# A recurrence and a mixer on one core: four turned tiles in the place of six, PE operations cut finer, loads shared between two queues, and new lists of order

## The chip, the cores and the metric

The kernel runs on one core of a Trainium2 chip. The metric is the device time of one execution in microseconds (us). Five engines work in parallel, each through its own list of instructions in order, and wait for each other by semaphores: TensorE (PE in the profile; PEld is its loading of weights), VectorE (DVE), ScalarE (ACT), GpSimd (POOL) and SyncE (SP), which only issues transfers. PE writes to PSUM, eight banks of 128 x 512 float32; DVE and ACT read it from there.

## The reference

```python
for t in range(S):                     # B, H, S, D = 4, 8, 768, 40
    y[:, :, t] = einsum('bhd,bhde->bhe', rt, state)
    Sa = einsum('bhde,bhe->bhd', state, at)
    state_decay = state * wt[:, :, None, :] - einsum('bhd,bhe->bhde', Sa, bt)
    state = state_decay + einsum('bhd,bhe->bhde', vt, kt)
x = y.transpose(0, 2, 1, 3).reshape(B, S, H * D)          # 4 x 768 x 320
theta = x @ w_theta
y = einsum('ts,bsd->btd', w_tok_r, x * cos(theta)) \
  + einsum('ts,bsd->btd', w_tok_i, x * sin(theta))
u = x + y
out = u + maximum(u @ w_ch, 0)
```

All inputs and the output are float32. Each head of each batch has a 40 x 40 state that runs through 768 steps; then a mixer over tokens and channels works on all heads of a batch together.

## The kernel before

The 768 steps of a batch are cut into 6 tiles of 128, so there are 24 tiles (i = 0 to 23, a batch after the other), and in each tile the recurrence is written as products of matrices. All 8 heads of a tile are worked on at once. The steps of tile i, by the names that the code gives its operations:

- `loads` (line 462): w, k, b, a, v of the tile into SBUF, as 1024 pieces of 160 bytes each. r of two tiles is loaded at once, in 256 pieces of 1280 bytes, "runs" of eight steps of a head. v is loaded in runs too for tiles 0 to 7 (`RUNS`, where the operation is called o), and k, b and a for the "turned" tiles 0 to 5 (`TURNED`). There are 25 loads of runs. All these loads are issued by SP.
- `prep` (line 503): logarithm of w on ACT, its running sums by a matmul with a triangle (`cs`; for tiles under `LATE` = 12 a second matmul gives the sums up to the step before), exponentials on ACT. In tiles that aren't turned, POOL multiplies k and b (`kb`, one operation of 640 columns) and a (`ah`) by these decays, and PE transposes the three (`tt`, 12 blocks, with v 16), which ACT or DVE copies out of PSUM (`et`) as features. In turned tiles POOL or ACT casts the raw runs (`ck`, `cb`, `ca`), PE transposes those (`tkbr`, `tar`) for two tiles at once, forms the sums transposed (`csT`), ACT takes two more exponentials of 512 columns (`xi`, `xw`), DVE makes the features by three products (`mk`, `mb`, `ma`), and PE transposes k and b back (`tbk`, copied by `ebk`).
- `attention_scores` (line 684): three products of features on half-arrays, each of 128 x 1024 results, which DVE multiplies by a mask (`mpsi`, `mphi`, `mlv`). The other way: ACT copies them with a sign and POOL sets the masked part to zero (`sel`). A fourth (`mlu`) follows from the recurrence.
- `recurrence` (line 694): `x0` adds the older state's part and the tile's own in one PSUM bank, `nx` copies it, `nu` continues in the same bank, `gt` forms the next state, which DVE scales (`egt`); `gd` and `nut` are transposes.
- `readout` (line 824): `y`, of the older state's part and two parts of scores, and DVE's product into x.
- The mixer: `theta` transposes x of two tiles, `sines` multiplies by w_theta, ACT takes sine and cosine, POOL or DVE makes the products z; `mix_row` is 6 chunks of 2 matmuls (`row`) over the tiles of a batch for each of its 6 rows, then the addition of x (`uadd`), a transpose, the channel product (`ch`) and the store.

A matmul works on the whole array of 128 rows or on half of it (64 rows, two at a time). `turn` (line 416) transposes by halves, `turn_whole` (line 422) by whole blocks; scores, `th3` and `ch3` use halves.

The program doesn't plan while it is built. Every operation is added to a list of 1390 with what it reads and writes; `ORDER` gives the order in which they are put on their engines, `HOMES` the PSUM banks, `PICK` (134 numbers) those which take their other form (ACT in the place of DVE or POOL, the other transpose, and so on), and `WARM` places matmuls on constants at the start. As every engine works in order, `ORDER` also sets what stands behind a waiting operation. The figures `cost` and `work` in the code have no part in what is built.

Of the kernel before, what the change touches and what calls it, by code (L numbers as in the profile page):

```python
# [19 lines left out]
TURNED = frozenset(range(6))  # L20
LATE = 12
ORDER = [
# [218 lines left out]
def mm(n):  # L241
    return max(n / 2.4 + 2.5, 25.0)
# [7 lines left out]
def kernel(  # L250
# [252 lines left out]
    def prep(i):  # L503
# [12 lines left out]
        def cs():  # L516
# [7 lines left out]
            if late:  # L524
                return
# [517 lines left out]
```

## Time and profile before

| | |
|---|---|
| time, median of 3 runs (lowest, highest) | 194.6 us (194.04, 196.16) |
| profiled execution: span from first to last instruction | 191.6 us |
| profiled execution: its own time | not given beside the span |
| mean granted PE clock | 0.991 |
| PE matmuls | 4223 |
| transfers | 30.90 MB in 110312 packets |

In the profile a line such as `L668 PE MATMUL ps<-feat ... x384 | 18.4, 221 | 1.9 <-ACT exi L611 0.9` is a group of instructions: line of the code, engine, operation, what it writes and reads, how often, busy us in all, mean ns of one, and the idle time of the engine just before them with what ended it. A line of a wait list gives who waited for whom: us in all, times, longest. A line of a table by stretch gives start and end, then the stretch's length and the busy us (and instructions) of PE, PEld, DVE, ACT and POOL, the granted clock, the DMA engines' busy share and GB/s. In the chain of work a piece is start, us, and what. The busy time of PE has modelled ends: matmuls overlap.

### The profile page before, as it was taken

To read this page: it belongs to the slowest core of one execution; us is meant where nothing else is said; L and a number is where in the kernel's file an instruction comes from. 1 tells how busy PE (TensorE), PEld (TensorE's weight loads), DVE (VectorE), ACT (ScalarE), POOL (GpSimd) and SP (SyncE) were. 2 spreads that over 40 slices of the span, in tenths; PEclk is the share of its full clock that TensorE was granted. 3 is DMA by queue.
4 is the path that set the end of the run, shared out by engine and by line. 5 is a ranking of instruction groups with operands and counts; after the bars stand their busy time and mean duration, and the time that the engine had idled before them with its cause. 6 is when DMAs were issued, how large, how long until landed. Compare 5 with 4: busy or idle time off the path is not lost.

```text
span 191.6 us, 9477 instructions
## 1 busy us (share of the span) xinstructions
PE 179.6 (94%) x4223; PEld 142.0 (74%) x4223; DVE 165.7 (86%) x268; ACT 157.9 (82%) x288; POOL 136.9 (71%) x162
## 2 busy tenths in 40 slices
PE   7679799999898999999999999999999999999992
PEld 7567587787687877788777787868877877876751
DVE  7599899998899998999889978998999998886552
ACT  3499999999999999989999979799999769883010
POOL 5584595496799789989989396694999983643200
PEclk9969999999999999999999999999999999999999
DMA  5999799989889999999997999999927011001131
GB/s 131 321 310 323 182 244 205 178 150 160 164 137 211 187 187 174 201 215 193 197 207 171 154 191 210 179 169 238 217 38 168 12 37 38 3 3 68 68 140 68
DMA packets 110312, 30.90 MB, mean 161 GB/s; under 512 B 98624, under 2 KB 110272, under 8 KB 110272
## 3 DMA queue, kind: packets, MB, share of 16 engines
q1 hardware_dynamic: 107840, 27.53, 66.6%
q0 software_dynamic: 2432, 2.77, 9.1%
q8 instruction: 33, 0.54, 1.1%
q14 instruction: 7, 0.06, 0.1%
HBM read 29.13 MB, written 3.93 MB: 173 GB/s over the span
## 4 chain that ended last, share of the span: by engine, by line
PE 74%; DVE 13%; ACT 7%; DMA 2%; issue 1%; SPq 1%; POOL 0%; ACTq 0%
PE ps L896 22%; PE ps L419 12%; PE ps L668 10%; PE ps L810 6%; DVE lam L676 4%; PE ps L842 4%; PE ps L424 3%; DMA raw_a<-in_a_dram 2%; PE ps L745 2%; PE ps L816 2%; PE ps L724 2%; PE ps L712 2%; PE ps L836 2%; PE ps L707 2%; PE ps L518 2%; DVE feat L625 2%
## 5 line engine op out<-in xcount | busy, mean ns | idle before, releaser
L676 DVE TENSOR_TENSOR lam<-ps,mask_p 128x1024 bf16<-128x1024 f32 x39 | 47.1, 1219 | 3.6 <-PE ps L668 3.3
L896 PE MATMUL ps<-z,wtok 128*128 128x320 bf16 x288 | 48.2, 299 | 0.0
L493 POOL TENSOR_TENSOR z<-cs,xp 128x640 bf16<-128x640 f32 x21 | 29.2, 1403 | 4.5 <-ACT cs L874 4.4
L896 PEld LDWEIGHTS <-wtok 128*128 128x128 bf16 x288 | 24.3, 97 | 9.1 <-issue 0.2
L493 POOL TENSOR_TENSOR kb<-raw_kb,ex 128x640 bf16<-128x640 f32 x18 | 25.8, 1433 | 2.0 <-ACT nx L718 1.3
L676 DVE TENSOR_TENSOR psi<-ps,mask_p 128x1024 bf16<-128x1024 f32 x19 | 23.1, 1219 | 1.1 <-PE ps L668 1.0
L668 PEld LDWEIGHTS <-feat 64*128 64x128 bf16 x576 | 18.0, 95 | 6.6 <-issue 4.4
L668 PE MATMUL ps<-feat 64*128 64x128 bf16 x384 | 18.4, 221 | 1.9 <-ACT exi L611 0.9
L676 DVE TENSOR_TENSOR phi<-ps,mask_n 128x1024 bf16<-128x1024 f32 x13 | 15.9, 1220 | 1.6 <-PE ps L668 1.6
L680 POOL TENSOR_SCALAR_AFFINE_SELECT phi<-phi 128x1024 bf16<-128x1024 bf16 x11 | 12.0, 1092 | 7.0 <-ACT phi L678 7.0
L842 PE MATMUL ps<-kb,lam 128*128 128x40 bf16 x384 | 15.5, 180 | 0.2 <-DVE lam L676 0.2
L452 ACT COPY feat<-ps 128x1024 f32<-128x1024 f32 (+1 forms) x14 | 14.0, 998 | 0.6 <-PE ps L419 0.5
L842 PEld LDWEIGHTS <-lam 128*128 128x128 bf16 x384 | 13.8, 96 | 0.8 <-issue 0.3
L642 ACT COPY rT<-ps 128x512 bf16<-128x512 bf16 x24 | 13.3, 600 | 0.3 <-PE ps L419 0.2
L509 ACT ACTIVATE lw<-raw_w 128x320 bf16<-128x320 f32 x24 | 11.4, 483 | 2.4 <-DMA raw_w<-in_w_dram 2.3
L680 POOL TENSOR_SCALAR_AFFINE_SELECT lam<-lam 128x1024 bf16<-128x1024 bf16 x9 | 9.8, 1090 | 4.9 <-ACT lam L678 4.9
L901 DVE TENSOR_TENSOR up<-ps,xp 128x320 bf16<-128x320 f32 x22 | 10.6, 487 | 2.8 <-PE ps L896 2.5
L493 POOL TENSOR_TENSOR ah<-raw_a,ex 128x320 bf16<-128x320 f32 x15 | 12.1, 806 | 0.7 <-ACT ex L544 0.4
L452 ACT COPY uT<-ps 128x320 f32<-128x320 f32 (+1 forms) x9 | 3.6, 404 | 10.8 <-PE ps L419 5.4
L678 ACT ACTIVATE phi<-ps 128x1024 bf16<-128x1024 f32 x11 | 11.4, 1033 | 1.0 <-PE ps L668 1.0
L836 PE MATMUL ps<-gd,rT 128*128 128x80 bf16 x80 | 12.2, 197 | 0.0
L728 ACT ACTIVATE nu<-ps 128x320 bf16<-128x320 f32 x24 | 10.8, 450 | 1.5 <-PE ps L724 1.2
(165 smaller groups left out, 538.4 us busy)
## 6 DMA issues: line engine op xcount, KB each, us to landing
raw_w<-in_w_dram SPq DMA_DIRECT2D x24, 160.0 KB, 4.7
raw_r<-in_r_dram SPq DMA_DIRECT2D x12, 320.0 KB, 5.0
out_dram<-oo SPq DMA_DIRECT2D x11, 320.0 KB, 3.1
raw_a<-in_a_dram SPq DMA_DIRECT2D x18, 160.0 KB, 4.5
raw_kb<-in_k_dram SPq DMA_DIRECT2D x18, 160.0 KB, 4.2
raw_kb<-in_b_dram SPq DMA_DIRECT2D x18, 160.0 KB, 4.4
raw_v<-in_v_dram SPq DMA_DIRECT2D x16, 160.0 KB, 5.0
raw_v<-in_v_dram SPq DMA_DIRECT2D x4, 320.0 KB, 5.7
```

The lines of the kernel that those rows point to most:

```text
L419: nc.tensor.transpose(out=dst[:, c, n * 64:n * 64 + 64], in_=block[rows(c)], identity=ident[rows(c), rows(c)])
L452: nc.scalar.copy(out=to, in_=source)
L493: pool = ("POOL", lambda: nc.gpsimd.tensor_tensor(out=dst, in0=in0, in1=in1, op=ALU.mult))
L509: add("ACT", "ln", i, lambda: nc.scalar.activation(out=heads(lw)[:, :, 0:D], in_=raw_w[s4], func=AF.Ln), 473, [("raw_w", s4)], [("lw", s2) ...
L642: add("ACT", "e" + nm, i + x, lambda x=x, dst=dst: nc.scalar.copy(out=dst.rearrange("p g (t q) -> p g t q", q=8), in_=ps(pr).bitcast(BF16) ...
L668: nc.tensor.matmul(t[:, q, g, :], lhsT=lhs[rows(q), g, :], rhs=rhs[rows(q), g, :], start=True, stop=True)
L676: add("DVE", kindm, i, lambda: nc.vector.tensor_tensor(out=flat, in0=whole(), in1=mask.to_broadcast([128, 2 * G, 128]), op=ALU.mult), 1217 ...
L680: add(None, "sel", i, None, 0, dkeys, dkeys, alts=(("POOL", lambda: nc.gpsimd.affine_select(out=flat, in_=flat, pattern=[[0, 2 * G], [1, 1 ...
L810: nc.tensor.matmul(ps(pk)[:, c, 0:DM], lhsT=lhs[:, 3 * c + kt, :], rhs=wt[:, 3 * c + kt, :], start=kt == 0, stop=False, skip_group_check=True)
L836: nc.tensor.matmul(t[:, g * 80:g * 80 + 80], lhsT=rT[:, g, :], rhs=gd[:, 2 * g:2 * g + 2, :], start=True, stop=False, skip_group_check=True)
L842: nc.tensor.matmul(t[:, h * D:h * D + D], lhsT=lam[:, n, p, g, :], rhs=kb[:, n, h, 0:D], start=first and n == 0, stop=n == 1, skip_group_c ...
L896: nc.tensor.matmul(ps(pk)[:, 0:DM], lhsT=wtok[t % NCH][:, c, s, :], rhs=z[:, c, s], start=s == 0 and c == 0, stop=s == NT - 1 and c == 1)
```

## The change

- `TURNED` holds tiles 0 to 3, not 0 to 5. Tiles 4 and 5 load k, b and a in pieces of 160 bytes and go the other way (products on POOL, `tt`).
- Operations of PE are cut finer, with the same matmuls: `tt` into a part for k and b, one for a and one for v; `cs` into its two matmuls' parts; `x0` into the tile's own part and the older state's (`x0s`); `gt` into the part of k and v (`gtk`) and the part of nu; `y` into `yv`, `ys` and `y`. There are 1512 operations.
- Loads of runs have a second form, issued by POOL. There are 22 of them now, and `PICK` takes this form for 13: r of tiles 2, 4, 6, 8, 10, 14, 16 and 18, v of tiles 0, 2, 4 and 6, a of tile 2.
- `ORDER`, `HOMES`, `PICK` (145 numbers) and `WARM` are new lists.
- Another way to cut the blocks of x and u (`SIDES`, `SLOT`) is in the code, for no tile: `SIDES` is empty.

```diff
-TURNED = frozenset(range(6))
+TURNED = frozenset(range(4))
+SIDES = frozenset()
...
-WARM = {14: (38, 0), 19: (10, 3), 20: (2, 3), 62: (4, 3)}
+WARM = {14: (38, 0), 20: (10, 0), 21: (2, 2), 64: (4, 4)}
...
-    def turn(dst, blocks):
-        for n, block in enumerate(blocks):
+    def turn(dst, blocks, at=0):
+        for n, block in enumerate(blocks, at):
...
+        if groups:
+            m = 0
+            for c, (count, keys) in enumerate(groups):
+                add("PE", kind + "abc"[c], i, lambda m=m, count=count: turn(
+                    ps(p).bitcast(BF16), blocks[m:m + count], m), reads=keys, writes=[p],
+                    at=at, new=(p, 2) if c == 0 else None, **quad_cost(4 * count))
+                m += count
...
             add("SP", "load" + nm, i, lambda to=raw, runs=runs: nc.sync.dma_start(
-                out=to, in_=runs), 600, [], [run_key(nm, i, 0), run_key(nm, i, 1)], work=1040)
+                out=to, in_=runs), 600, [], [run_key(nm, i, 0), run_key(nm, i, 1)], work=1040,
+                alts=(("POOL", lambda to=raw, runs=runs: nc.gpsimd.dma_start(
+                    out=to, in_=runs)),))
...
-            if late:
-                return
+
+        def earlier():
             before = lw[:, LEAD - 1:LEAD - 1 + H * 64].rearrange("p (h x) -> p h x", x=64)
...
+        if not late:
+            add("PE", "csx", i, earlier, mm(328), [("lw", s2)], [pk], tail=tail(328))
...
-        skeys, dkeys = [("kb", i % NKB), ("ah", i % 3)], list(parts)
+        groups, dkeys = [(8, [("kb", i % NKB)]), (4, [("ah", i % 3)])], list(parts)
...
         def x0():
             t = ps(pk)
+            for h in range(H):
+                nc.tensor.matmul(t[:, h * D:h * D + D], lhsT=psi[:, h % 2, h // 2, :],
+                                 rhs=vb[:, h, 0:D], start=h == 0, stop=True,
+                                 skip_group_check=True)
+
+        def carried():
+            t = ps(pk)
             for g in range(G):
...
+                nc.tensor.matmul(t[:, g * 80:g * 80 + 80], lhsT=feat[:, 8 + g, :],
+                                 rhs=gt_old[:, g, :, 0:D], start=False, stop=True,
+                                 skip_group_check=True)
+        add("PE", "x0", i, x0, 8 * 25, [("psi", i % NSC), ("v", i % NRV)], [pk], new=(pk, 1),
+            tail=tail(40))
+        if not first:
+            add("PE", "x0s", i, carried, 4 * mm(80), [("fa", st), ("gt", (i + 1) % 2)], [pk],
+                tail=tail(80))
...
+            add("PE", "gtk", i, lambda: gains(kb[:, 0], vb, True),
+                4 * mm(80) + (mm(320) if join else 0), [("kb", i % NKB), ("v", i % NRV)] +
                 ([("gt", (i + 1) % 2)] if join else []), [gk], new=(gk, 1), tail=tail(80))
+            add("PE", "gt", i, lambda: gains(kb[:, 1], nu, False), 4 * mm(80),
+                [("kb", i % NKB), ("nu", s2)], [gk], tail=tail(80))
...
+        add("PE", "yv", i, lambda: y(0), 8 * 25, [("lam", s2, 0), ("kb", i % NKB)], [pk],
+            new=(pk, 1), tail=tail(40))
+        if not first:
+            add("PE", "ys", i, carried, 4 * mm(80), [("rT", i % 6), ("gd", (i + 1) % 2)], [pk],
+                tail=tail(80))
+        add("PE", "y", i, lambda: y(1), 8 * 25, [("lam", s2, 1), ("kb", i % NKB)], [pk],
+            tail=tail(40))
```

The new lists, from the start of the list of order on, begin for SP with w0, b0, k0, a0, w1, r0, w2, k2, w3, b2, w4 and for POOL, behind the casts of tile 0's b and k, with the loads of v of tile 0, a of tile 2 and v of tile 2.

More of the change, by code (lines that the diff above doesn't have):

```diff
@@ L427, in quad_cost, with turned @@
         return dict(mode=64, tail=tail(64), cost=n * 8)
-    def turned(kind, kinde, i, blocks, skeys, dst, dkeys, at="tile", eng="ACT", part=64):
+    def turned(kind, kinde, i, blocks, skeys, dst, dkeys, at="tile", eng="ACT", part=64,
+               groups=()):
         p = ("ps", kind, i)
@@ L432, in turned @@
         whole = n <= 8
-        add("PE", kind, i, lambda: turn(ps(p).bitcast(BF16), blocks), reads=skeys, writes=[p],
-            at=at, new=(p, 2), alts=(("PE", lambda: turn_whole(ps(p).bitcast(BF16), blocks)),)
-            if whole else (), **quad_cost(4 * n))
+        if groups:
[5 more added lines that the diff above has]
+                m += count
+        else:
+            add("PE", kind, i, lambda: turn(ps(p).bitcast(BF16), blocks), reads=skeys,
+                writes=[p], at=at, new=(p, 2),
+                alts=(("PE", lambda: turn_whole(ps(p).bitcast(BF16), blocks)),)
+                if whole else (), **quad_cost(4 * n))
         def places(width, source):
@@ L528, in cs @@
                              rhs=before[:, :, 0:D + 1], start=True, stop=True)
-        add("PE", "cs", i, cs, (1 if late else 2) * mm(328) + 4 * 25, [("lw", s2)], [pk],
-            new=(pk, 1 if late else 2), tail=tail(2 if late else 328))
+        add("PE", "cs", i, cs, mm(328) + 4 * 25, [("lw", s2)], [pk],
+            new=(pk, 1 if late else 2), tail=tail(2))
+        if not late:
+            add("PE", "csx", i, earlier, mm(328), [("lw", s2)], [pk], tail=tail(328))
         if late:
@@ L704, in x0 @@
             t = ps(pk)
-            for g in range(G):
-                if not first:
-                    nc.tensor.matmul(t[:, g * 80:g * 80 + 80], lhsT=feat[:, 8 + g, :],
-                                     rhs=gt_old[:, g, :, 0:D],
-                                     start=g == 0, stop=False, skip_group_check=True)
-                for p in range(2):
-                    h = 2 * g + p
-                    nc.tensor.matmul(t[:, h * D:h * D + D], lhsT=psi[:, p, g, :],
-                                     rhs=vb[:, h, 0:D], start=first and h == 0,
-                                     stop=True, skip_group_check=True)
-        add("PE", "x0", i, x0, 8 * 25 + (0 if first else 4 * mm(80)),
-            [("fa", st), ("psi", i % NSC), ("v", i % NRV)] +
-            ([] if first else [("gt", (i + 1) % 2)]), [pk], new=(pk, 1), tail=tail(40))
+            for h in range(H):
[4 more added lines that the diff above has]
+            t = ps(pk)
+            for g in range(G):
+                nc.tensor.matmul(t[:, g * 80:g * 80 + 80], lhsT=feat[:, 8 + g, :],
[6 more added lines that the diff above has]
+                tail=tail(80))
         add("ACT", "nx", i, lambda: nc.scalar.copy(out=nx, in_=ps(pk)[:, 0:DM]),
@@ L773, in recurrence, with blocks_of @@
                nuT_t[i % 2], [("nuT", i % 2)])
-    def blocks_of(t):
+    def blocks_of(t, sides=False):
+        if sides:
+            split = t.rearrange("p (c k d) -> p k c d", c=2, d=64)
+            return [split[:, kt] for kt in range(5)]
         return [t[:, m:m + 128] for m in range(0, t.shape[1], 128)]
@@ L797, in mixed, with sides @@
         pk = ("ps", kind, q)
+        if not alone(q) and q in SIDES:
+            def sides():
+                for kt in range(5):
+                    for c in range(2):
+                        nc.tensor.matmul(ps(pk)[:, c, 0:DM], lhsT=lhs[rows(c), kt, :],
+                                         rhs=wt[rows(c), SLOT[c][kt], :], start=kt == 0, stop=kt == 4,
+                                         skip_group_check=True)
+            add("PE", kind, q, sides, 5 * mm(320), [lkey] + wkeys, [pk], at=at, new=(pk, 2),
+                tail=tail(320), mode=64)
+            return
         if alone(q):
```

48 lines of the change are left out of this document (21 added, 27 removed), and 212 rows, old and new, of tables (HOMES, ORDER, PICK).

## The prediction

> **What bounds the kernel now.** I read the page first, then busy time by stretch, then who waited for whom in each stretch, then the chain of work.
>
> ```profile
> span 191.6 us, 9477 instructions
> PE 179.6 (94%) x4223; PEld 142.0 (74%) x4223; DVE 165.7 (86%) x268; ACT 157.9 (82%) x288; POOL 136.9 (71%) x162
> 0.00:10.00 10.00, 7.29 (x124) 6.45 (x124) 6.34 (x44) 4.48 (x7) 5.77 (x21) 1.00 0.81 230
> 10.00:68.50 58.50, 53.13 (x1500) 43.99 (x1501) 55.60 (x73) 56.88 (x111) 43.37 (x52) 0.97 1.01 204
> 68.50:187.00 118.50, 118.06 (x2597) 91.09 (x2593) 102.74 (x150) 96.26 (x171) 87.73 (x91) 1.00 0.67 138
> PE ps L419 <- DVE us L901: 0.4, 1, 0.4
> 68.51 0.20 PE L707 MATMUL ps<-gt,feat 128*128 128x80 bf16 x1
> ```
>
> By the page TensorE (PE) is 94% busy, but that is a mean over two different stages. The stretches (columns: PE, PEld, DVE, ACT, POOL busy, granted clock, DMA share) part them. From 68.5 to 187 PE is busy for 118.06 of 118.5 us, and the wait list of that stretch for PE has one entry, 0.4 us: nothing but the amount of PE work sets its length. From 10 to 68.5 PE idles 5.4 us while ScalarE (ACT) is busy 56.88 of 58.5 and VectorE (DVE) 55.60; GpSimd (POOL) idles 15.1. I cut at 68.5 because there PE begins tile 9's state product (line 707), a point found in both lists of order.
>
> ```profile
> ACT exw L613 <- DVE feat L628: 1.0, 1, 1.0
> ACT ex L544 <- PE ps L527: 0.3, 1, 0.3
> POOL phi L680 <- ACT phi L678: 5.9, 4, 2.9
> POOL r L499 <- DMA raw_r<-in_r_dram: 1.4, 1, 1.4
> 8.09 0.47 ACT L509 ACTIVATE lw<-raw_w 128x320 bf16<-128x320 f32 x1 [1.02 <-DMA raw_w<-in_w_dram]
> ```
>
> In the early stretch ACT's longest wait is 1.0 us, once: it works through its list almost without pause, and PE gets results at ACT's pace. So the end is, nearly, the time at which ACT reaches tile 9, plus the PE work behind that point, plus 4.6 us of tail. Work taken from ACT ahead of tile 9 is worth its full length; work taken from PE counts behind tile 9; the rest is covered.
>
> **PE work.** The finer operations issue the same matmuls as before (12 for a state product, 20 for an output, 8 for a state update). Three things do change.
>
> ```profile
> 102.22 0.33 PE ps L668 x8
> 110.97 0.22 PE ps L668 x8
> 109.62 0.56 PE ps L896 x4
> 115.52 0.65 PE ps L896 x4
> 123.38 1.13 PE ps L419 x70
> L604 PE MATMUL ps<-ntri_inc,lw 128*128 128x128 bf16 x24 | 2.3, 219 | 0.0
> ```
>
> These are pieces of the chain. Eight score matmuls on half-arrays (64 rows) take 0.33 us behind whole-array matmuls and 0.22 behind half-array ones; four mixing matmuls take 0.65 against 0.56. So each change between the two array modes costs PE some 0.10 us. Reading both lists in order, PE changes mode 166 times before and 172 after: +0.6 us. The Trainium skill, TensorEngine Tiling (Array Packing), Key Properties, says that changing the tiling mode drains TensorE; it speaks against cutting operations finer, states no price, and the rows agree on the direction. Two tiles fewer are turned: 40 blocks (80 half transposes) go and 24 blocks (48) come, 32 x 16 ns (1.13 us for 70) = -0.5 us, and 8 of line 604's matmuls go. Each costs between 28 ns (0.22 us for eight of the same width on half-arrays) and its own length of 219; I take twice 28, since they fill the whole array: -0.45. Whole-array transposes are picked 33 times, not 32: +0.1. Sum -0.25 us, between -1.6 and 0; behind tile 9, where no tile is turned and the lists hold nearly the same PE work, I count -0.1.
>
> **ACT and DVE ahead of tile 9.** I counted each kind of operation that the two lists put ahead of that point.
>
> ```profile
> L613 ACT ACTIVATE exw<-ps,sign_col 128x512 f32<-128x512 f32 x6 | 4.2, 698 | 1.2 <-DVE feat L628 1.0 <-PE ps L745 0.2
> L611 ACT ACTIVATE exi<-ps 128x512 f32<-128x512 f32 x6 | 3.6, 601 | 0.0
> L678 ACT ACTIVATE phi<-ps 128x1024 bf16<-128x1024 f32 x11 | 11.4, 1033 | 1.0 <-PE ps L668 1.0
> L452 ACT COPY nuT<-ps 128x256 f32<-128x256 f32 x15 | 5.6, 376 | 1.0 <-PE ps L419 0.9
> L452 ACT COPY feat<-ps 128x768 f32<-128x768 f32 (+1 forms) x2 | 1.8, 916 | 0.2 <-PE ps L419 0.2
> L452 ACT COPY gd<-ps 128x160 f32<-128x160 f32 x9 | 2.8, 312 | 0.6 <-PE ps L419 0.4 <-PE ps L424 0.2
> L452 ACT COPY xT<-ps 128x320 f32<-128x320 f32 x7 | 3.1, 436 | 0.4 <-PE ps L419 0.4
> L718 ACT CAST nx<-ps 128x320 bf16<-128x320 f32 x24 | 10.4, 434 | 1.3 <-PE ps L712 1.0
> L874 ACT ACTIVATE cs<-ps 128x640 f32<-128x640 f32 (+1 forms) x13 | 8.7, 666 | 2.6 <-PE ps L801 2.6
> L625 DVE TENSOR_TENSOR feat<-ps,exi 128x512 bf16<-128x512 bf16 x12 | 7.9, 682 | 1.6 <-PE ps L419 1.6
> L456 DVE COPY kb<-ps 128x1024 bf16<-128x1024 bf16 x4 | 2.7, 680 | 0.0
> L676 DVE TENSOR_TENSOR phi<-ps,mask_n 128x1024 bf16<-128x1024 f32 x13 | 15.9, 1220 | 1.6 <-PE ps L668 1.6
> L456 DVE COPY nuT<-ps 128x512 bf16<-128x512 bf16 x9 | 3.8, 419 | 0.6 <-PE ps L419 0.6
> L456 DVE COPY wtok<-ps 128x1536 bf16<-128x1536 bf16 x2 | 1.9, 948 | 0.0
> ```
>
> ACT loses the two exponentials of tiles 4 and 5 (2 x 0.698 + 2 x 0.601 = 2.6), three score copies net (3.1), three copies of nuT (1.1), two of gd (0.6) and a logarithm (0.47); it gains three feature copies (3 x about 0.8 = 2.4, below the mean of two sizes), three casts of 640 columns, which ACT never does in this trace (between 0.434 for 320 columns and twice that; 0.7 each, 2.2), and a sine and a copy of xT (0.7 + 0.4): -2.2 us in instruction lengths. Lengths overlap: over the whole list they add up to 178 us against 157.9 busy, a factor 0.89, so **-1.95 us**. One of the casts (tile 0's a) can stand in the 1.02 us hole ahead of tile 2's logarithm at 8.09, for a further **-0.6** (0 if the cast is late itself). DVE loses six decay products and two copies (5.5), two copies of wtok (1.9) and one of xT (0.4, taken as ACT's); it gains three score products (3.7), three copies of nuT (1.3) and two of gd (0.6, as ACT's), and one of its feature copies is a larger one (about 0.2): -2.0. It falls with ACT, so it doesn't take ACT's place.
>
> **POOL and the loads.** Tiles 4 and 5 now need kb and ah products on POOL.
>
> ```profile
> L493 POOL TENSOR_TENSOR kb<-raw_kb,ex 128x640 bf16<-128x640 f32 x18 | 25.8, 1433 | 2.0 <-ACT nx L718 1.3
> L493 POOL TENSOR_TENSOR ah<-raw_a,ex 128x320 bf16<-128x320 f32 x15 | 12.1, 806 | 0.7 <-ACT ex L544 0.4
> L499 POOL CAST z<-raw_kb 128x640 bf16<-128x640 f32 x6 | 4.3, 723 | 2.9 <-DMA raw_kb<-in_k_dram 1.6 <-DMA raw_kb<-in_b_dram 1.2
> L680 POOL TENSOR_SCALAR_AFFINE_SELECT phi<-phi 128x1024 bf16<-128x1024 bf16 x11 | 12.0, 1092 | 7.0 <-ACT phi L678 7.0
> L946 POOL DMA_DIRECT2D wrow<-in_moe_w_tok_i_dram x6 | 3.5, 585 | 0.0
> q1 hardware_dynamic: 107840, 27.53, 66.6%
> ```
>
> Ahead of tile 9 POOL gains three kb (4.3), two ah (1.6) and ten issues of loads (10 x 0.585 = 5.9), and loses five casts (3.6), two selections (2.2) and a weight load (0.6): **+5.4 us**. Its 15.1 idle us of the early stretch cover that; if its waits for ACT stay as long as they are, up to 5.4 is late. Behind an issue on POOL stand casts and products that PE needs, but an issue has little to wait for: each of the 13 writes a fresh buffer or one whose last reader is an earlier cast on POOL itself, but for r of tile 14, which follows a cast on ACT. On SP, w, k, b and a move up past the loads taken out; its queue is in order, so they are issued earlier. Tiles 4 and 5 come in pieces of 160 bytes: 6144 small packets for 768 large ones, the same bytes. At q1's mean (66.6% of 191.6 us over 107840 packets) 5376 more packets are at most +6.4 us of DMA time and at least none. The DMA share is already 1.01, yet past 17 us only one wait of 1.4 us ends with a load, so I take 0; without that lead it would be up to 6.4.
>
> **The tail.** Before, three chunks of the last row follow the last chunk of row 22 and cover its addition; after, one does.
>
> ```profile
> 186.32 0.49 DVE L901 TENSOR_TENSOR us<-ps,xs 128x320 bf16<-128x320 f32 x1 [0.32 <-PE ps L896]
> ```
>
> A chunk is two matmuls (half of 0.56, 0.28 us), so 0.49 - 0.28 = 0.2 us of the first addition pushes the second: +0.2.
>
> **Sum.** 191.6 - 1.95 - 0.6 - 0.1 + 0.2 = 189.15 us of span. The median of the runs shown, 194.6, is 3.0 above the span; the profiled run's own time isn't given, so I take 3.0 for what lies around: **192.2 us**, 1.2% less.
>
> **The rivals.**
> (a) *The early stretch keeps its length.* DVE's 55.60 of 58.5 is nearly ACT's load, and the new order may leave holes on ACT where there were hardly any: the 2.55 us saved are idle. 191.6 + 0.1 + 3.0 = 194.7. For it: two engines near 95%; against it: both get lighter by 2 us.
> (b) *The finer operations pay beyond ACT's list.* PE no longer stops a whole state product for the older state, and ACT, idle 5.5 of the first 10 us, starts sooner; half of that gone gives 192.2 - 2.8 = 189.4. Against it: behind 10 us ACT has only 1.6 us left to win.
> (c) *GpSimd becomes the pacer* (slower). The 5.4 us come in front of the kb and ah products of tiles 4 to 9, which PE's transposes and so the scores wait for. If half of its waits for ACT stay, tile 9 comes 2.7 us later than before: 197.3; if all stay, 200. It decides from the point where POOL's idle time up to tile 9 can't shrink by 5.4. For it: 5.9 us of POOL's idle are waits for ACT's score copies; against it: 15.1 is nearly three times what is needed.
> (d) *Issues on GpSimd are held by DVE.* If each load waited out a DVE score product, 10 x 1.22 = 12.2 us more in front of tile 9, less the rest of the idle time (15.1 - 5.4): 2.5 us late in the place of 2.55 early, 194.6 + 2.5 = 197.1. The trace speaks against it: issues of 0.585 us beside a DVE that is 95% busy. The Trainium skill, SBUF — State Buffer, SBUF: two separate sides, says that a two-port DVE operation locks GpSimd out of writing descriptors; by its figure, about 0.62 us alone and 3.1 overlapped, ten issues would cost some 25 us, and the time would be near 210 (an estimate).
>
> **Numbers.** Chances: forecast 0.45, (a) 0.22, (b) 0.14, (c) 0.16, (d) 0.03. A measurement of this kernel can tell about 1% from no change, so faster means below 192.65 and slower above 196.55. The forecast's own bounds (casts, hole, PE's -1.6 to 0) are about 190.5 to 194; two thirds of it, all of (b) and a little of (a) are faster: 0.45. Slower are (c), (d) and the end of (a) with late loads: 0.20. The range runs from 188.5, below (b), to 197.0, into (c).
>
> **What would show it.** Right: tile 9's line of state products begins near 66 us; ACT is still above 95% in the stretch before it, with fewer exponentials; PE has no wait worth naming behind it; PE's busy time is about the same. (a): ACT idle inside the early stretch rises by 2 us. (b): ACT is busy clearly over 4.5 us in the first 10. (c): PE's or DVE's waits name POOL kb or ah, and POOL's idle stays near 15. (d): issues on POOL longer than 1 us. Also wrong if the late stretch shows PE waits: then the new order, not the work, sets the end.

## The result and the profile after

| kernel | executions | median us | against the kernel before |
|---|---|---|---|
| before | 4 | 194.32 (193.91 to 196.16) | |
| changed | 4 | 199.45 (198.81 to 200.0) | 1.0267 [1.0204, 1.0329], slower |
| changed, again | 10 | 196.24 (194.28 to 198.92) | 1.0055 [1.0006, 1.0104] |
| changed, third time | 6 | 196.91 (195.19 to 199.81) | 1.0105 [1.0048, 1.0162] |

The forecast was 192.2 us. The change makes the kernel slower, but by less than the first four executions say: its executions scatter, and the first four all lay at the upper end. The ratios leave out executions that the measurement counts as disturbed; wherever a mean stands below, all executions are in it. Over all 20 the changed kernel has a mean of 197.29 us, the kernel before 194.83 over the 110 beside the experiments: 2.46 us, 1.3%.

The page of the changed kernel's first profile (span, then busy time of each engine, then the granted clock in 40 slices):

```profile
span 197.1 us, 9389 instructions
PE 181.6 (92%) x4178; PEld 140.4 (71%) x4178; DVE 163.4 (83%) x262; ACT 157.8 (80%) x285; POOL 146.1 (74%) x173
PEclk9995899999999699999999999999999999999998
```

Two dips stand in the clock, in the 4th and 5th slice and in the 14th. The trace has them as TensorE at half clock from 14.3 to 21.1 us and from 65.5 to 68.9; the kernel before has one such spell, from 11.0 to 14.4 (what dips in the tail is left out here). The stretches (PE, PEld, DVE, ACT, POOL busy, granted clock, DMA share), cut where tile 9's state product begins:

```profile
0.00:10.00 10.00, 7.66 (x130) 6.80 (x131) 6.43 (x45) 5.52 (x9) 7.00 (x23) 1.00 0.82 216
10.00:72.80 62.80, 54.36 (x1399) 43.65 (x1399) 53.24 (x69) 55.72 (x104) 48.45 (x59) 0.92 1.03 195
72.80:191.30 118.50, 117.93 (x2639) 89.19 (x2635) 101.39 (x145) 96.52 (x174) 90.66 (x94) 1.00 0.67 136
```

In order of time, the first matmuls of tile 9's state product (start, length):

```profile
72.78 0.35 PE L730 MATMUL ps<-v,psi 128*128 128x40 bf16 x8
```

Tile 9 starts at 72.8 and not at 68.5: 4.3 of the 5.5 us by which the span grew are lost ahead of it. Behind it PE is as busy as before, 117.93 of 118.5 us, but what follows tile 9's start is 1.2 us longer. In the early stretch ACT was busy for 56.88 of 58.5 us; now it is busy for 55.72 of 62.8, so it idles 7.1 us in the place of 1.6. PE's waits there, then ACT's and POOL's:

```profile
PE ps L429 <- POOL o L521: 1.8, 1, 1.8
PE ps L692 <- ACT ex L568: 1.4, 2, 1.0
PE ps L771 <- issue: 1.1, 2, 0.7
PE ps L737 <- issue: 1.0, 1, 1.0
ACT feat L666 <- PE ps L429: 1.6, 1, 1.6
ACT nx L745 <- PE ps L737: 1.2, 3, 0.8
POOL psi L704 <- ACT psi L702: 4.6, 2, 3.5
POOL o L521 <- DMA raw_v<-in_v_dram: 2.4, 1, 2.4
```

PE waits 1.8 us for POOL's cast of tile 0's values, and POOL 2.4 us for their load. Two more stands of PE, 1.1 and 1.0 us, wait for nothing that the profile names ("issue"); they lie in the middle of an operation. In order of time, POOL's start and those stands:

```profile
5.30 0.72 POOL L521 CAST z<-raw_kb 128x640 bf16<-128x640 f32 x1 [1.72 <-DMA raw_kb<-in_b_dram]
6.21 0.72 POOL L521 CAST z<-raw_kb 128x640 bf16<-128x640 f32 x1 [0.20 <-DMA raw_kb<-in_k_dram]
6.88 0.88 POOL L503 DMA_DIRECT2D raw_v<-in_v_dram  x1
13.16 0.72 POOL L521 CAST o<-raw_v 128x640 bf16<-128x640 f32 x1 [2.45 <-DMA raw_v<-in_v_dram]
13.93 0.41 PE L429 MATMUL ps<-ident,o 64*128 64x64 bf16 x16 [1.75 <-POOL o L521]
59.60 0.21 PE L771 MATMUL ps<-v,kb 128*128 128x80 bf16 x1 [0.66 <-issue]
65.25 0.28 PE L737 MATMUL ps<-gt,feat 128*128 128x80 bf16 x3 [0.95 <-issue]
```

The load of tile 0's values is issued at 6.88 us, behind two casts of POOL that wait for loads themselves; in the kernel before SP issues it at 4.02. The two later stands end 1.4 us after a packet of 16 KB on the queue of instructions has landed (at 58.19 and 63.87 us in the trace). Between the two, and from the stand at 54.23 us to the first of them, lie 256 and 255 matmuls and loads of weights, so one such packet seems to hold 256 of PE's instructions (every matmul has a load of weights of its own).

```profile
q8 instruction: 32, 0.52, 1.1%
```

### The profile page after: what moved, and what is told of

Same layout as the page of the kernel before. It is cut to its first block, busy times and chain, and to the rows that moved or that the text cites. A ratio compares the mean times of both kernels' runs of the same rounds, so it can differ in the third digit from the quotient of the medians.

```text
span 197.1 us, 9389 instructions
## 1 busy us (share of the span) xinstructions
PE 181.6 (92%) x4178; PEld 140.4 (71%) x4178; DVE 163.4 (83%) x262; ACT 157.8 (80%) x285; POOL 146.1 (74%) x173
## 4 chain that ended last, share of the span: by engine, by line
PE 75%; ACT 7%; POOL 4%; DVE 4%; issue 4%; DMA 3%; SPq 2%; POOLq 0%
PE ps L941 21%; PE ps L429 11%; PE ps L692 11%; PE ps L851 6%; PE ps L876 4%; PE ps L771 3%; PE ps L751 3%; PE ps L434 3%; DMA raw_r<-in_r_dram 3%; PE ps L730 3%; PE ps L857 2%; PE ps L540 2%; PE ps L883 1%; PE ps L737 1%; DVE psi L700 1%
## 5 line engine op out<-in xcount | busy, mean ns | idle before, releaser
L941 PE MATMUL ps<-z,wtok 128*128 128x320 bf16 x288 | 50.2, 300 | 0.0
L515 POOL TENSOR_TENSOR kb<-raw_kb,ex 128x640 bf16<-128x640 f32 x20 | 28.6, 1433 | 3.6 <-ACT ex L557 1.8
L700 DVE TENSOR_TENSOR phi<-ps,mask_n 128x1024 bf16<-128x1024 f32 x19 | 23.2, 1220 | 4.5 <-PE ps L692 4.3
L700 DVE TENSOR_TENSOR psi<-ps,mask_p 128x1024 bf16<-128x1024 f32 x16 | 19.4, 1217 | 0.3
L515 POOL TENSOR_TENSOR ah<-raw_a,ex 128x320 bf16<-128x320 f32 x20 | 16.2, 809 | 1.9 <-ACT ex L568 1.4
L876 PEld LDWEIGHTS <-lam 128*128 128x128 bf16 x384 | 13.4, 96 | 1.7 <-issue 0.2
L894 DVE TENSOR_TENSOR xp<-ps,ex 128x320 bf16<-128x320 f32 x22 | 10.6, 486 | 3.5 <-PE ps L876 3.4
L704 POOL TENSOR_SCALAR_AFFINE_SELECT psi<-psi 128x1024 bf16<-128x1024 bf16 x8 | 8.7, 1093 | 4.7 <-ACT psi L702 4.6
L755 ACT ACTIVATE nu<-ps 128x320 bf16<-128x320 f32 x24 | 10.7, 444 | 1.9 <-PE ps L751 1.9
L704 POOL TENSOR_SCALAR_AFFINE_SELECT lam<-lam 128x1024 bf16<-128x1024 bf16 x10 | 12.1, 1214 | 0.0
L745 ACT CAST nx<-ps 128x320 bf16<-128x320 f32 x24 | 10.3, 430 | 2.2 <-PE ps L737 1.7
L790 POOL TENSOR_TENSOR gt<-exw,ex 128x320 bf16<-128x320 f32 x8 | 5.9, 740 | 7.5 <-DVE exw L786 7.5
```

Source lines behind the costliest of these rows:

```text
L515: pool = ("POOL", lambda: nc.gpsimd.tensor_tensor(out=dst, in0=in0, in1=in1, op=ALU.mult))
L700: add("DVE", kindm, i, lambda: nc.vector.tensor_tensor(out=flat, in0=whole(), in1=mask.to_broadcast([128, 2 * G, 128]), op=ALU.mult), 1217 ...
L704: add(None, "sel", i, None, 0, dkeys, dkeys, alts=(("POOL", lambda: nc.gpsimd.affine_select(out=flat, in_=flat, pattern=[[0, 2 * G], [1, 1 ...
L755: add("ACT", "enu", i, lambda: nc.scalar.mul(out=nu[:, :, 0:D], in_=ps(pk)[:, 0:DM].rearrange("p (h d) -> p h d", h=H), mul=-1.0), 437, [p ...
L876: nc.tensor.matmul(t[:, h * D:h * D + D], lhsT=lam[:, n, h % 2, h // 2, :], rhs=kb[:, n, h, 0:D], start=n == 0 and h == 0, stop=True, skip ...
L941: nc.tensor.matmul(ps(pk)[:, 0:DM], lhsT=wtok[t % NCH][:, c, s, :], rhs=z[:, c, s], start=s == 0 and c == 0, stop=s == NT - 1 and c == 1)
```

## The experiments

**Which part of the change.** The first four undo one thing each or fill one gap.

```diff
 # e1_loads_sp: all 13 loads of runs back on SP's queue, at their places in the list
-PICK = [2, 8, 9, 12, ..., 941, ...]   # the 13 loads taken out of PICK
 # e2_three_sp: only v of tile 0 and a, v of tile 2
-PICK = [2, 9, 12, ...]                # these three taken out
 # e3_fill: constant matmuls ahead of the transposes of tile 0's values (operation 31)
-WARM = {14: (38, 0), 20: (10, 0), 21: (2, 2), 64: (4, 4)}
+WARM = {14: (38, 0), 20: (10, 0), 21: (2, 2), 64: (4, 4), 31: (24, 4)}
 # e4_fine_only: the new code, but six turned tiles and the lists of the kernel before,
 # each cut operation's pieces one behind the other at the place of the whole
-TURNED = frozenset(range(4))
+TURNED = frozenset(range(6))
```

> The changed kernel with all 13 loads of runs back on SP; nothing else differs. Theory L (the loads on GpSimd: v of tile 0 is issued at 6.88 us, before at 4.02, PE stands 1.97 us for it and the clock is at half for 6.8 us): the start recovers, the tile 9 point comes some 2.5 us earlier, time near 197.0. Theory I (PE's instruction refills land late: 0.86 and 1.15 us inside operations of tiles 7 and 8, and the half clock at 65.5 us that follows): the start gains 1 to 2 us, but the stalls near 58 and 64 us stay, time 197.5 to 199. Theory O (the order itself leaves ScalarE with holes): within 1 us of the changed kernel, 198.5 to 200.

> The changed kernel with only the first three loads that GpSimd issues (v of tile 0, a and v of tile 2) back on SP, the other ten stay. Theory L says that lateness at the start is what costs: as with all 13 back, near 197.0, within 0.5 us of it. If GpSimd's time for issuing is what costs (ten issues of 0.6 us ahead of tile 9), it stays 1.5 us or more behind the kernel with all 13 back. Theory O: 198.5 to 200.

> The changed kernel with 24 matmuls on constants put into PE's wait of 1.97 us ahead of tile 0's transposes of v; the load stays late. They keep PE busy there and shift every later instruction refill by 48 instructions. If the half clock from 14.3 us on is what makes the start dear, the clock stays at 1.0 there and 1 to 1.5 us are gained, near 198. If the stand itself is, nothing is gained, 199 to 200. Theory I: the stalls inside operations near 58 and 64 us move to other operations or vanish; if they vanish with the half clock behind them, up to 3 us are gained, 196.5.

> The kernel before with the finer operations alone: six turned tiles, all loads on SP, the order, banks and choices of before, each cut operation's parts put one behind the other. PE's matmuls and changes of array mode are those of before. Theories L, I and O all say: same as before, 193.8 to 195. If cutting costs by itself (more waits and signals on PE), 196 or more.

Measured: e1 218.73 us, 1.1255 [1.1175, 1.1334]; e2 202.33, 1.0399 [1.0332, 1.0466]; e3 194.39, 0.9995 [0.9961, 1.003]; e4 194.33, 1.0013 [0.9971, 1.0056].

Neither e1 nor e2 is a clean undo: in SP's queue, which is in order, the loads stand behind loads that wait for a free buffer. In e2 tile 2's a comes so late that POOL waits 8.6 us for it (e2's waits), and PE stands 5.87 us inside an operation behind POOL (e2 in order of time):

```profile
POOL z L521 <- DMA raw_a<-in_a_dram: 8.6, 1, 8.6
```

```profile
24.46 0.61 PE L429 MATMUL ps<-ident,z 64*128 64x64 bf16 x16 [5.87 <-POOL z L521]
```

So with this list, loads on GpSimd help; SP alone would be much worse. e4 says that the finer cutting by itself is worth nothing that can be measured. e3 gets the whole loss back with 24 matmuls that compute nothing, although tile 0's values come no earlier: their transposes begin at 13.9 us in e3's trace as in the changed kernel's. No half-clock spell is left in its span. But 24 matmuls, with their loads of weights, also move every later refill of PE's instructions by 48.

**Clock, late values or refills.**

```diff
 # e5_fill_late: 16 matmuls ahead of tile 4's lower triangle product, at 47.8 us
+WARM[320] = (16, 2)
 # e6_o0_sp: v of tile 0 loaded by SP, right behind r of tile 0
-PICK = [2, ...]
-ORDER = [..., 5, 2, 19, 6, 21, 27, 1, 7, ...]
+ORDER = [..., 5, 19, 6, 21, 27, 1, 2, 7, ...]
 # e7_wide: 6 matmuls of 512 columns where e3 has 24 of 128
+WARM[31] = 6 of 512 columns
 # e8_before_fill: the kernel before, 16 matmuls ahead of tile 0's first psi product
+WARM[41] = (16, 3)
```

> The changed kernel with 16 constant matmuls (128 columns each, about 0.9 us of PE time if nothing covers them) put ahead of tile 4's lower triangle product, where PE stood 1.04 us waiting for DVE in the changed kernel. Nothing ahead of 47.8 us is touched, so the half clock from 14.3 to 21.1 us and the late values of tile 0 stay. Theory 1 (the loss is PE's instruction refills landing late in the two operations at 58.7 and 64.1 us, and their place among the loads hangs on how many PE instructions stand before them): the two stalls of 0.8 and 1.1 us go or shrink, the second half-clock spell (65.5 to 68.9 us) goes with them, and the time comes to 196.5 to 198. Theory 2 (the loss is the half clock and the late values in the first 21 us): the time stays within 199 to 200. Theory 3 (the list's order itself, whatever PE does between): 199 to 200.5.

> The changed kernel with one load moved: the values of tile 0 are loaded by SP, right behind tile 0's r, and not by GpSimd behind its own work. No constant matmul is added. Theory 1 (PE's stand of 1.94 us at 12 us, for tile 0's values, starts the half clock and sets the chain): the values land about 2 us earlier, their transposes begin near 12 rather than 13.9 us, the half clock from 14.3 us does not come or is 3.4 us and not 6.8, and the time comes to 195 to 197. Theory 2 (refills alone): the instructions ahead of the refills are the same, so the time stays at 198.5 to 200. Theory 3 (SP's queue gives what GpSimd's takes: a load more in SP's line pushes the later ones): 199 to 202.

> The changed kernel with 6 constant matmuls of 512 columns ahead of the transposes of tile 0's values, in the place where 24 of 128 columns brought 194.4 us: about as much PE time, but 6 matmuls and not 24, so that PE's instruction refills fall at nearly the same operations as in the changed kernel. Theory 1 (the clock kept up by a busy PE is what the 24 brought): the granted clock is 1.0 from 6 to 65 us and the time is 194 to 196. Theory 2 (what they brought is the shift of the refills by 24 matmuls): the stalls inside the operations near 58 and 64 us come back and the time is 197 to 199.

> The kernel before with 16 constant matmuls (128 columns) ahead of tile 0's first psi product, where PE stood 0.87 us and where its one half-clock spell, 11.0 to 14.4 us, begins. Theory 1 (half clock on the path of the early stretch costs time): the spell goes, PE's 3.4 us at half clock become about 1.7 us of work, and the time falls by 0.5 to 1.7 us, to 193 to 194. Theory 2 (ACT paces the early stretch and the clock of PE is covered): within 0.4 us of the kernel before, 194.3 to 195. A fill that lies in the way would give 195 to 196.

Measured: e5 198.04 us (195.06 to 202.17), 1.0087 [1.0034, 1.014]; e6 196.95 (194.38 to 197.54), 1.0062 [1.001, 1.0113]; e7 194.74, 1.0027 [0.9986, 1.0067]; e8 195.89, 1.007 [1.0036, 1.0103].

e7 speaks for the clock: its ten executions have a clock of 0.994 to 1.0, with a quarter of the instructions. Their mean is 195.13 us, where the changed kernel's own five executions at a clock of 0.99 or above lie too (195.09); e3's is 194.16, so a part of what e3 brings may be the place of the refills. e8 shows that the kernel before gains nothing from such a fill: the spell is gone from its trace, and it is slower. PE's waits from 24 to 80 us say where that goes, into stands for "issue":

```profile
PE ps L419 <- issue: 1.3, 1, 1.3
PE ps L668 <- issue: 1.1, 1, 1.1
PE ps L842 <- issue: 0.7, 1, 0.7
```

The kernel before has two in that stretch:

```profile
PE ps L527 <- issue: 0.5, 1, 0.5
PE ps L419 <- issue: 0.3, 1, 0.3
```

So with 16 matmuls more these stands are 2.3 us longer, and tile 9 begins 1.7 us later, at 70.2. That the matmuls are the reason is not shown: it is one trace each, and the unaltered changed kernel has such stands in two of its traces and not in the third (e15, below).
 e6 gives a part back: the values arrive, but SP's next load is late in turn, w of a later tile, and ACT stands for it:

```profile
L531 ACT ACTIVATE lw<-raw_w 128x320 bf16<-128x320 f32 x2 | 0.9, 472 | 2.5 <-DMA raw_w<-in_w_dram 2.5
```

e5 showed what none of the theories had said: up to 47 us it is the changed kernel, yet the execution that was profiled had no half-clock spell and took 195.06 us, while the others went up to 202.17. So the changed kernel itself was run again.

**The same kernel, and the refills.**

```diff
 # e9_after_again, e15_after_third: the changed kernel, nothing edited
 # e10_shift, e16_shift_again: the opening in wide matmuls, 29 matmuls fewer
-WARM = {14: (38, 0), ...}
+WARM = {14: 9 of 512 columns, ...}
 # e11_wide_shift: e10 and e7 together
 # e12_sp_wide: e6, and wide matmuls ahead of operations 42 (4), 31 (2) and 115 (4)
 # e13_after_bare: without the 16 constant matmuls in the gaps
-WARM = {14: (38, 0), 20: (10, 0), 21: (2, 2), 64: (4, 4)}
+WARM = {14: (38, 0)}
 # e14_before_bare: the same in the kernel before
-WARM = {14: (38, 0), 19: (10, 3), 20: (2, 3), 62: (4, 3)}
+WARM = {14: (38, 0)}
```

> The changed kernel unaltered, as the yardstick on the chip of the runs beside it. If half-clock spells of TensorE make the loss, its executions scatter with their granted clock: those at 0.97 near 199.5 us, any at 0.99 or above near 196 to 197. If the loss is fixed in the list's order, all lie within 198.5 to 200.5 whatever the clock.

> The changed kernel with the 38 opening constant matmuls of 128 columns replaced by 9 of 512 columns: the same PE time ahead of the first real work, but 29 PE instructions fewer, so that every later refill of PE's instructions falls 29 instructions away from where it fell, about as far as the 24 matmuls moved it the other way. No gap is filled. Theory 1 (the clock in the gap at 12 us): time and clock as the changed kernel beside it, 198 to 200 us at 0.97 to 0.98. Theory 2 (the place of the refills): the stalls inside operations near 58 and 64 us go, and the time is 195 to 197.

> The same opening, together with the 6 constant matmuls of 512 columns that fill the gap at 12 us: against the run with those 6 alone (194.7 us at a clock of 0.994 to 1.0) only the place of the refills differs, by 29 instructions. It prices that place at an undisturbed clock. Theory 1: 193.8 to 195.8, the same within 1 us, with the clock at 0.994 to 1.0. Theory 2: a new set of stalls, 196 to 198, or the stalls that are left in the late stretch (0.75 us in an operation at 85 us, 0.55 at 76 us in the runs so far) go and it falls below 194.

> Both remedies together: tile 0's values loaded by SP behind its r, and constant matmuls of 512 columns in the three places where PE stood in that run: 4 ahead of tile 0's first psi product (1.04 us idle), 2 ahead of the transposes of tile 0's values, 4 ahead of tile 2's k, b, r products (2.36 us idle inside them). Theory 1 (clock, plus 1.8 us of earlier values): the clock stays at 0.994 to 1.0 and the time is 193 to 194.7, below both kernels if the earlier values count. Theory 2 (a load more in SP's line delays what stands behind it, and the 2.36 us in tile 2 stay): 195 to 196.5 in spite of the clock.

> The changed kernel without the 16 constant matmuls that it already has in PE's gaps between 6 and 9 us (the opening 38 stay): PE idles some 1.2 us more there. Theory 1 (PE's idle time in the first 20 us makes half-clock spells likelier, and the changed order pays for each): the mean granted clock falls below that of the unaltered kernel beside it (0.987 on the chip before), to 0.97 to 0.98, and the mean time rises to 197.5 to 200. Theory 2 (the spells come by chance whatever PE does): clock and time as the unaltered kernel beside it, within 0.003 and 0.7 us.

> The kernel before without its 16 constant matmuls in the same gaps. Theory 1: its clock falls likewise (from 0.988 to 0.975 to 0.983), but its early stretch is paced by ACT, so it pays about 0.8 us and not 1.8 us for each 0.01 of clock: 195 to 196. Rival (every kernel pays alike for half clock): 196.5 to 198. Theory 2: 194.3 to 195.3 at a clock of 0.985 to 0.99.

> The changed kernel unaltered once more: the first four executions lay at 199.45 us with a clock of 0.968 to 0.979, ten others at 196.2 with 0.974 to 1.0. If time goes with the clock, the executions here fall on the same line: about 194.4 us at a clock of 1.0 and 1.8 us more for each 0.01 below it, whatever their number at each clock. If not, something else changed between the two, and the times at one clock differ by more than 1.5 us.

> The kernel with the opening of 9 wide constant matmuls (29 PE instructions fewer) again, beside the unaltered one. If the place of the refills is what the 29 instructions moved: 0.5 to 1 us below the unaltered kernel at the same clock, with no stall inside an operation at 57 to 63 us, and 194 to 195 us in all; if the 194.2 of the first look was luck of the clock, the two kernels agree within 0.5 us at one clock.

Measured: e10 194.22 us, 0.9986 [0.9954, 1.0017]; e16 194.14, 0.9976 [0.9939, 1.0014]; e11 194.68, 0.9978 [0.9935, 1.0021]; e12 196.16, 1.0052 [1.0013, 1.009]; e13 196.07 (193.31 to 199.58), 1.0006 [0.9958, 1.0053]; e14 194.84, 1.0031 [0.9987, 1.0075]; e9 and e15 stand in the first table.

e9 is the strongest comparison of the study, since nothing differs but the execution. Its early stretch, to be read against the changed kernel's above:

```profile
10.00:69.20 59.20, 51.42 (x1402) 41.60 (x1400) 52.95 (x70) 54.88 (x105) 47.63 (x57) 1.00 1.01 198
```

In order of time, PE's wait for tile 2's cast, its stands inside an operation, and the start of tile 9:

```profile
18.33 0.41 PE L429 MATMUL ps<-ident,z 64*128 64x64 bf16 x16 [1.05 <-POOL z L521]
57.70 0.21 PE L771 MATMUL ps<-v,kb 128*128 128x80 bf16 x1 [0.94 <-issue]
62.80 0.28 PE L737 MATMUL ps<-gt,feat 128*128 128x80 bf16 x3 [0.40 <-issue]
69.24 0.35 PE L730 MATMUL ps<-v,psi 128*128 128x40 bf16 x8
```

The span is 193.2 us, 3.9 shorter, and 3.5 of that is there at tile 9, with the clock whole throughout. The stands near 58 and 63 us are there in both, 1.3 us here and 1.6 in the first profile. The difference comes in two steps. Tile 1's state product begins at 22.6 us in the first profile and at 20.8 in e9; between tile 8's and tile 9's, 8.9 us pass there and 7.2 here: the 65.5 to 68.9 us spell lies between, and 0.55 us of it is the stand, 0.95 us there and 0.40 here. For the first step neither cause is enough alone: e3 has the values as late (13.9 us) at a whole clock, and tile 1 begins at 21.0; e13's profile has 6.8 us of half clock, from 13.1 to 19.9, but the values earlier (12.5), and tile 1 begins at 21.2. By these traces PE's wait for tile 2's cast (1.05 us at 18.33 in e9) takes up the one or the other; the two together go past it, and cost 1.8. e6 fits that: with the values early its times do not go with the clock, 196.52 us at 0.99 or above (4 executions), 196.31 from 0.98 to 0.99 (4), 196.66 below (2).

All executions sorted by their granted clock, mean us (number):

| | clock 0.99 to 1 | 0.98 to 0.99 | below 0.98 |
|---|---|---|---|
| before (110) | 194.38 (45) | 195.05 (54) | 195.60 (11) |
| changed (20) | 195.09 (5) | 197.08 (8) | 199.11 (7) |
| gap filled, e3 and e7 (20) | 194.65 (20) | | |
| 29 matmuls fewer, e10 and e16 (22) | 193.82 (12) | 194.78 (8) | 196.25 (2) |

At a nearly whole clock the changed kernel is 0.7 us behind the kernel before; at a low clock 3.5. A line through the 20 gives 1.81 us for each 0.01 of clock (standard error 0.25), one through the 110 gives 0.70 (0.12). 0.01 of 197 us is about 2 us of full-speed PE time, so the changed kernel pays nearly all of what the clock loses, the kernel before a third. The bare kernels point to PE's idle time as what brings the spells: with the 16 matmuls gone the mean clock falls from 0.982 to 0.974 in the changed kernel and from 0.988 to 0.978 in the one before. The time didn't follow in e13 (mean 196.19 us; 197.5 to 200 was expected): spells ahead of 20 us, alone, cost little in its trace, as told above. But 16 matmuls fewer also move its refills, and no run parts the two. In e14 the mean rose to 195.36, as the first theory had it.

e10 and e16 come from the refills' side. Their traces show no stand above 0.4 us inside an operation behind 24 us, the 22 executions have a mean of 194.39 us, and at one clock they lie 1.3 us or more below the changed kernel. They have 29 matmuls fewer, which are 58 instructions with the loads of weights, and not 29. That the number of PE instructions ahead matters is shown; how it does is not settled. e11, which has the same opening, has new stands (1.06 and 0.63 us at 48 and 58 us) and gains nothing over e7; e5, moved by 16 matmuls at 47.8 us, is slower than the changed kernel at the same clock (197.38 us in its five executions at 0.99 or above), which nothing here explains; and e15's trace, of the unaltered kernel, has no stand near 58 and 63 us, though it has two spells. A stand lowers PE's use as well, and so the clock; the runs don't part the two. e12, which joins the two remedies, is no better (a mean of 197.11 us): its fills come on top of SP's late loads.

No version beats the kernel before by more than can be told: the best, e10 and e16, are 0.1 to 0.2% below it.

## Why the prediction was wrong

**The step that failed** is "the end is, nearly, the time at which ACT reaches tile 9", with "work taken from ACT ahead of tile 9 is worth its full length". The work did leave ACT, and in the size forecast. An undisturbed execution of the new order (e10's first 10 us and early stretch):

```profile
0.00:10.00 10.00, 7.78 (x101) 4.61 (x102) 6.45 (x45) 5.54 (x9) 7.05 (x23) 1.00 0.83 224
10.00:68.20 58.20, 50.72 (x1398) 41.12 (x1399) 52.94 (x69) 54.03 (x104) 46.40 (x56) 1.00 1.04 199
```

What ACT waited for in that stretch of e10:

```profile
ACT ex L568 <- PE ps L549: 1.0, 1, 1.0
ACT feat L472 <- PE ps L429: 0.8, 2, 0.6
ACT nuT L472 <- PE ps L434: 0.5, 1, 0.5
ACT v L677 <- PE ps L429: 0.5, 1, 0.5
```

Up to tile 9 ACT is busy for 5.54 + 54.03 = 59.57 us; before, 4.48 + 56.88 = 61.36: -1.8, against -1.95 forecast. But tile 9 begins at 68.2, only 0.3 earlier. The saved time is idle time of ACT, most of it behind PE's products: 4.2 us behind 10 us in the place of 1.6. That is what rival (a) says. That its 194.7 also meets the undisturbed executions (195.09 at a clock above 0.99, 193.82 with the refills moved) is partly luck, since two of its terms are off by about 1 us each and cancel: what lies around the span, and what follows tile 9's start.

An engine that is busy 97% of a stretch was taken for its pacer. The chain of the kernel before, which goes back at each step to what was waited for, says otherwise. Adding up its pieces from 10 to 68.5 us gives ACT 10.5, DVE 22.5 and PE 23.2 us. From 20.8 to 39 us it runs almost only through DVE; two pieces of it:

```profile
34.49 1.22 DVE lam L676
35.71 2.26 DVE psi L676 x2
```

So work taken from ACT did not lie on that chain for the most part. In e10 the same sum, to 68.2 us, gives ACT 13.4, PE 15.2, POOL 14.4, DVE 2.2 and a load 7.9; in e9 POOL has only 0.7. The engines take turns, each nearly full, and the order decides who waits. PE's two longest waits in e10's stretch name ACT and POOL:

```profile
PE ps L692 <- ACT ex L568: 1.6, 2, 1.1
PE ps L429 <- POOL z L521: 1.4, 1, 1.4
```

Why the new order opens holes about as long as the work taken out is argued from these chains and not shown by a run.

**The loads, 0:** the prediction has the loads left on SP issued earlier, and takes nothing for them. Tile 2's b is issued earlier, at 8.00 us in e10 against 8.55, but it lands later. Its cast on POOL, before and then in e10, and the load in e10's chain:

```profile
15.51 1.39 POOL L499 CAST z<-raw_kb 128x640 bf16<-128x640 f32 x2 [1.17 <-DMA raw_kb<-in_b_dram]
18.00 0.72 POOL L521 CAST z<-raw_kb 128x640 bf16<-128x640 f32 x1 [1.83 <-DMA raw_kb<-in_b_dram]
8.00 9.95 DMA raw_kb<-in_b_dram
```

That cast begins at 15.5 to 16.0 us in the four traces of the old order and at 16.9 to 18.2 in twelve of the new one (all but e1 and e2); PE's wait for POOL's z above is for it. POOL issues four loads of its own between 6.9 and 10.7 us, which may be what slows this one. No run moves it, so its share of the lost time is open.

**The hole at 8.09, -0.6:** filled. ACT is busy for 5.52 us of the first 10, not 4.48, and the gain is lost in the later holes.

**PE behind tile 9, -0.1, and the tail, +0.2:** from tile 9 to the end 191.6 - 68.5 = 123.1 us before; 197.1 - 72.8 = 124.3 after, 124.0 in e9, 124.2 in e10. So +0.9 to +1.2 where +0.1 was forecast. To the end of the last row's matmuls it is 117.8 us before and 118.3 to 118.6 in these three, +0.5 to +0.8; the tail behind them is 5.3 before and 5.7, +0.4. The prediction took two copies of the token weights away from DVE ahead of tile 9, but left out PE's transposes that go with them: these stand behind tile 9 now (the weights' transposes from there on, before and changed).

```profile
L419 PE MATMUL ps<-ident,wrow 64*128 64x64 bf16 x48 | 1.0, 190 | 0.0
L429 PE MATMUL ps<-ident,wrow 64*128 64x64 bf16 x96 | 2.1, 190 | 0.0
```

That is 1.1 us more; against it four matmuls of `sines` went the other way, 0.7 us less (`wth,xT`, 6.4 and 5.7 us). e4, with the finer operations in the old order, is level with the kernel before, so the order and not the cutting pays.

**DVE, -2.0:** 6.34 + 55.60 = 61.94 before, 6.43 + 53.24 = 59.67 after: -2.3. It didn't take ACT's place; it lost its own in the chain, as told above.

**POOL, +5.4, covered:** 5.77 + 43.37 = 49.14 before, 7.00 + 48.45 = 55.45 after: +6.3. Rival (c) needed PE or DVE waiting for POOL's kb and ah products; PE's wait for kb is 0.2 us, 0.4 in e10. Yet POOL, which has no piece of the early chain before, has 14.4 us of it in e10, so a part of (c) is not excluded. And PE waited for POOL's cast of tile 0's values, which the prediction didn't see: it asked what an issue on POOL waits for, not what stands ahead of it. Two casts that wait for loads do, 2.9 us of delay (6.88 against 4.02).

**Rival (d):** an issue of a load on POOL takes 0.72 to 0.88 us in those lines, beside 0.585 for an issue of weights before; the weights' issues still take 0.577, which suggests another form of load and not a hold-up. The Trainium skill, SBUF — State Buffer, SBUF: two separate sides, has a transfer from GpSimd take some 3.1 us in the place of 0.62 while VectorE locks it out; no issue here is stretched like that.

**What no term held:** half-clock spells, and PE standing for instructions. The page of before had both in sight: a mean clock of 0.97 in the early stretch, and waits for "issue" in PE's list. They cost less there (0.70 us for each 0.01 of clock), and so they were read as harmless in the new order too. The sum also took 3.0 us for what lies around the span; it is 1.7 (198.81 - 197.1), and the rest was the scatter of executions.

## What to carry to other kernels

Ask of an engine that is busy 97% of a stretch whether it sets the pace or takes turns with others, and add up the chain of work by engine to see: work taken off an engine that is seldom in the chain turns into idle time unless the others' results come earlier too. When work moves to the other side of a point in the list, move its part on every engine in the sum. When loads move to another queue, look at what is queued ahead of the first of them there, above all in the first 15 us, when each cast waits for a load. And run a kernel whose executions scatter more than once before explaining a difference: sort them by the granted clock, and compare at equal clocks.

## What was not expected of the hardware

**The clock goes by windows.** The half-clock spells last 3.4 or 6.8 us, and their edges lie on a grid of 3.4 us whose phase differs from one execution to the next. Cutting the traces on each one's grid shows what comes ahead of a spell. In the changed kernel's first profile (a window each; the column behind the length is PE's busy time):

```profile
7.50:10.91 3.41, 2.15 (x50) 1.70 (x43) 2.96 (x5) 2.83 (x6) 3.08 (x5) 1.00 1.12 313
10.91:14.32 3.41, 1.42 (x54) 1.13 (x55) 3.08 (x4) 1.89 (x5) 1.16 (x2) 1.00 1.08 319
14.32:17.73 3.41, 3.00 (x60) 2.24 (x54) 1.70 (x2) 3.12 (x7) 1.66 (x4) 0.50 1.18 282
62.10:65.51 3.41, 2.10 (x70) 1.70 (x65) 3.19 (x6) 2.67 (x4) 3.37 (x4) 1.00 1.21 243
```

Two windows of e9:

```profile
9.53:12.94 3.41, 2.05 (x62) 1.63 (x61) 3.28 (x5) 3.33 (x7) 2.34 (x4) 1.00 1.11 345
12.94:16.35 3.41, 2.85 (x87) 2.13 (x77) 3.41 (x4) 3.41 (x9) 1.74 (x3) 1.00 1.10 307
```

And the one ahead of e16's only spell, 20.8 to 24.2 us:

```profile
17.38:20.79 3.41, 1.96 (x56) 1.41 (x52) 2.36 (x5) 2.74 (x5) 2.79 (x5) 1.00 1.01 207
```

Half clock followed windows with PE busy for 1.42, 1.96 and 2.10 us of 3.41, whole clock windows with 2.05, 2.15 and 2.85. So the line runs near 60% and isn't sharp: 2.10 us brought a spell and 2.05 didn't (in other traces of the study windows of 1.87, 1.91 and 1.98 us stayed without a spell, and the window at 14.32, busy for 3.00 us at half clock, was followed by one more). Whether PE's gaps at 10 to 14 us fall into one window or are parted by an edge depends on that phase. That this is what scatters the times is a reading; no run set the phase. The Trainium skill, TensorE: Matmul & The Clock Gate, What's actually happening, tells of a free-running window of about 3.4 us; these traces agree. The Trainium skill, TensorE: Matmul & The Clock Gate, Why this matters for your kernels, asks for no idle gap above some 3 us; in the changed kernel's first profile the longest wait of PE ahead of a spell was 1.8 us, and several short ones in one window were enough.

**PE can stand for its own instructions.** Stands of 0.4 to 1.3 us inside an operation, 256 matmuls and loads of weights apart in the first profile, end 1.3 to 1.7 us after a 16 KB packet has landed (e9, e11 and e8 too), at a DMA share of about 1. The Trainium skill, Runtime: NRT & Kernel Launch, Instruction fetch mechanics, has the blocks of 16 KiB and calls their cost mostly hidden; here two or three in a run were not, 3.1 us in e8.
